# The start of an attention and gMLP kernel: first norms by a ScalarE root and a VectorE reciprocal, V weights in two pieces behind three chunks of x, turns woven into the first V passes

## Chip, cores, metric

One core of one Trainium2 chip. The metric is the device time of the whole kernel in microseconds (us). A run has a time and a mean granted TensorE clock (1.000 is full rate). Below, "T1" is the eight 128x128 transposes ("turns") of chunk 1 of x; a "pass" is one matmul of 512 columns; "wv a" and "wv b" are the two pieces of the V weights; "the fifth pass" is the first that needs wv b; "the first q pass" is the first matmul with the q weights, which follows all of the first V passes. TensorE takes its instructions in a fixed order, and so does each other engine.

## The reference

Layer norm of x, an attention with memory over four segments, a second layer norm and a gated MLP, 2048 rows of 1024. Only its first steps matter here: the norm of rows 0 to 511 (chunks 0 to 3 of 128 rows) and their product with the first 512 columns of wv.

```python
def _layernorm(x, axis=-1, eps=1e-05):
    m = jnp.mean(x, axis=axis, keepdims=True)
    v = jnp.var(x, axis=axis, keepdims=True)
    return (x - m) / jnp.sqrt(v + eps)
...
    x = A_x
    h = x + _A_ref(_layernorm(x, axis=-1), A_wq, A_wk, A_wv, A_wo, A_beta)
    h2 = h + _B_ref(_layernorm(h, axis=-1), B_w_in, B_w_sp, B_b_sp, B_w_out)
# in _A_ref: v = x @ wv, q = x @ wq, k = x @ wk, ...
```

## The kernel before

Every operation is recorded first. A list scheduler then lays down a fixed order for ScalarE (ACT), VectorE (DVE), GpSimd (POOL) and the DMA queue from assumed costs, while TensorE keeps the order of the program text. Its figures decide orders only; all times below are the chip's. These are the parts that the change touches:

```python
    N_WARM = 10
    AT = [5, 6, 6, 9]
    TCOPY = [(DVE, DVE), (ACT, ACT), (ACT, ACT), (DVE, ACT)]
    ...
    for k in range(N_WARM):
        mm(PS[:, 7, :], ZERO[:, 0:128], ZERO[:], True, True)
    ...
    for h in range(2):
        x_cols(0, h)                      # chunk 0 in two halves
    dma(XIN[1][:], x2d[128:256, :])
    wv_rows(0, 4)                         # wv a
    dma(XIN[2][:], x2d[256:384, :])
    wv_rows(4, 8)                         # wv b
    ...
    # layernorm(): bn_stats twice and bn_aggr on VectorE, then
        if start:
            ts1(RS[k][:], MV[k][:, 1:2], LN_EPS, ALU.add, fast=1)
        else:
            pts1(RS[k][:], MV[k][:, 1:2], LN_EPS, ALU.add)
        ptt(RS[k][:], RS[k][:], MHALF[:], ALU.pow)              # GpSimd
        ts(dst, src, MV[k][:, 0:1], RS[k][:], ALU.subtract, ALU.mult)
    ...
    # layernorm_act() (chunk 1): sum and sum of squares on ScalarE, then add and pow on GpSimd
    ...
    x_turn_pe(0)
    for tcl in range(4):
        b = bank()
        for i in range(8):
            if i == AT[tcl] and tcl < 3:
                x_turn_pe(tcl + 1)
            mm(b[:], XNT[0][:, i, tcl * 128:(tcl + 1) * 128], WV[:, i, 0:512], i == 0, i == 7)
        act(V[0][:, tcl, 0:16, 0:32], b.rearrange("p (h d) -> p h d", d=32), ACTF.Copy)

    for k, d in ((first[2], turned[0][1]), (first[2] + 1, first[1] + 4), (first[3], first[2] + 3),
                 (first[3] + 1, first[2] + 5)):
        G.ops[k].deps.add(d)              # e.g. chunk 2's first statistic behind chunk 0's copies
    Pq(0)
```

`AT[0] = 5` puts T1 behind chunk 0's fifth pass; `TCOPY` says which engine copies each half of a turn out of PSUM.

The softmax here doesn't subtract the row's maximum and nothing guards it: scores larger than these inputs give would overflow.

## Time and profile before

| | before |
|---|---|
| time, first three runs | 797.02 us median (796.05 to 797.2) |
| span of the profiled run | 795.0 us |
| TensorE busy | 789.5 us (99%) |
| wv b landed | 9.28 us |
| fifth pass starts | 9.32 us |
| first q pass starts | 16.97 us |

The span counts from the first to the last instruction. TensorE has hardly anything left to give, so the place to read is the chain of waits at the start. The lines are in the prediction below, with how to read them.

### The profile page before, as it was taken

How to read it: one execution, taken by the hardware profiler on the slowest of the kernel's cores; microseconds unless marked ns; L12 is line 12 of the kernel's file. 1: busy time of each engine (PE TensorE's matmuls, PEld its weight loads, DVE VectorE, ACT ScalarE, POOL GpSimd, SP SyncE). 2: the span in 40 equal slices, each digit the busy share in tenths (PEclk: the TensorE clock that was granted, in tenths of full speed). 3: DMA queues.
4: the chain of work that ended last, by engine and by line, in shares of the span. 5: the costliest groups of instructions: out<-in, count | busy, mean ns of one | idle time of the engine just before them, and what ended most of it. 6: DMA issues, size and time to landing. Idle time of an engine off the chain costs nothing.

```text
span 795.0 us, 12074 instructions
## 1 busy us (share of the span) xinstructions
PE 789.5 (99%) x5376; PEld 321.6 (40%) x4773; DVE 369.8 (47%) x853; ACT 288.6 (36%) x338; POOL 140.8 (18%) x270
## 2 busy tenths in 40 slices
PE   8999999999999999999999999999999999999998
PEld 3454554555554542341322414443244334424433
DVE  5773788768765686704215051132233223322322
ACT  4788977777778862132323323100000000000000
POOL 2463535433443341100001010000000000000000
DMA  9757524632523658420000116703310530011001
GB/s 307 156 123 172 137 47 95 136 68 68 87 55 87 173 117 216 145 53 1 1 0 1 28 33 157 187 1 82 105 33 1 119 100 1 0 54 60 0 1 54
DMA packets 128471, 64.77 MB, mean 81 GB/s; under 512 B 95520, under 2 KB 120352, under 8 KB 128416
## 3 DMA queue, kind: packets, MB, share of 16 engines
q1 hardware_dynamic: 128416, 63.99, 32.7%
q8 instruction: 40, 0.66, 0.3%
q14 instruction: 15, 0.12, 0.1%
HBM read 32.51 MB, written 8.39 MB: 51 GB/s over the span
## 4 chain that ended last, share of the span: by engine, by line
PE 99%; DMA 1%; SPq 0%; issue 0%; DVE 0%
PE ps L327 81%; PE ps L328 14%; PE ps L459 3%; DMA wv<-in_A_wv_dram 1%; SPq L511 0%; PE ps L463 0%; DVE hx L490 0%
## 5 line engine op out<-in xcount | busy, mean ns | idle before, releaser
L327 PE MATMUL ps<-wspT,z 128*128 128x512 bf16 x896 | 194.0, 379 | 0.0
L468 ACT ACTIVATE e<-ps 128x2048 bf16<-128x2048 f32 x80 | 149.8, 1873 | 40.0 <-PE ps L459 40.0
L327 PEld LDWEIGHTS ps<-wspT,z 128*128 128x128 bf16 x896 | 87.7, 98 | 106.4 <-issue 1.0
L468 ACT ACTIVATE z<-ps 128x512 bf16<-128x512 f32 x120 | 63.1, 571 | 145.4 <-PE ps L327 145.4
L490 DVE TENSOR_TENSOR tg<-ps,brow 128x512 bf16<-128x512 f32 x56 | 38.7, 691 | 150.2 <-PE ps L327 122.1
L693 POOL TENSOR_SCALAR_AFFINE_SELECT e<-e 128x1024 bf16<-128x1024 bf16 (+1 forms) x80 | 77.5, 969 | 122.5 <-ACT e L468 122.3
L327 PE MATMUL ps<-hnT,win 128*128 128x512 bf16 x448 | 97.3, 379 | 0.0
L328 PE MATMUL ps<-win,hnT 128*128 128x512 bf16 (+1 forms) x384 | 90.1, 344 | 0.0
L327 PE MATMUL ps<-wout,y 128*128 128x512 bf16 (+2 forms) x252 | 85.8, 367 | 0.0
L561 DVE BATCH_NORM_STATS2 stats<-z 128x6 f32<-128x448 bf16 x64 | 40.1, 627 | 96.6 <-ACT z L468 95.0
L490 DVE TENSOR_TENSOR hx<-hx,ps 128x512 bf16<-128x512 bf16 (+1 forms) x65 | 42.2, 673 | 81.7 <-PE ps L327 81.5
L328 PE MATMUL ps<-wout,y 128*128 128x512 bf16 x210 | 79.6, 379 | 0.0
L327 PEld LDWEIGHTS ps<-hnT,win 128*128 128x128 bf16 x448 | 43.9, 98 | 54.1 <-issue 2.0
L327 PE MATMUL ps<-wv,xnT 128*128 128x512 bf16 x256 | 60.7, 379 | 1.6 <-DMA wv<-in_A_wv_dram 1.3
L327 PE MATMUL ps<-xnT,wk 128*128 128x512 bf16 (+2 forms) x264 | 60.8, 374 | 0.0
L327 PE MATMUL ps<-xnT,wq 128*128 128x512 bf16 x256 | 60.8, 380 | 0.0
L327 PE MATMUL ps<-wo,oT 128*128 128x512 bf16 x256 | 58.8, 379 | 0.0
L327 PEld LDWEIGHTS ps<-wout,y 128*128 128x128 bf16 x252 | 24.2, 98 | 72.2 <-issue 69.1
L327 PE MATMUL ps<-win,hnT 128*128 128x512 bf16 x128 | 48.5, 379 | 0.0
L327 PEld LDWEIGHTS ps<-win,hnT 128*128 128x128 bf16 x128 | 12.5, 98 | 81.4 <-issue 80.9
L327 PEld LDWEIGHTS ps<-v,e 128*128 128x128 bf16 x1280 | 40.1, 96 | 9.8 <-issue 1.5
L327 PE MATMUL ps<-v,e 128*128 128x33 bf16 x1280 | 42.1, 177 | 0.0
(69 smaller groups left out, 604.3 us busy)
## 6 DMA issues: line engine op xcount, KB each, us to landing
win<-in_B_w_in_dram SPq DMA_DIRECT2D x6, 1024.0 KB, 5.7
hx<-in_A_x_dram SPq DMA_DIRECT2D x16, 256.0 KB, 3.0
out_dram<-hx SPq DMA_DIRECT2D x16, 256.0 KB, 2.3
hx<-out_dram SPq DMA_DIRECT2D x16, 256.0 KB, 2.8
out_dram<-hx SPq DMA_DIRECT2D x31, 128.0 KB, 1.7
xin<-in_A_x_dram SPq DMA_DIRECT2D x15, 256.0 KB, 5.2
wout<-in_B_w_out_dram SPq DMA_DIRECT2D x2, 1792.0 KB, 10.4
wq<-in_A_wq_dram SPq DMA_DIRECT2D x2, 1024.0 KB, 7.5
```

The source lines that it names most:

```text
L327: return e.matmul(out, lhsT, rhs, start=start, stop=stop)
L328: return e.add_instruction(mybir.InstMatmult(name="I-%d" % (1000000 + o.idx), engine=e.engine, ins=[e.lower_ap(rhs), e.lower_ap(lhsT)], ou ...
L459: G.op(PE, lambda e: e.matmul(o, lhsT, rhs, start=True, stop=True, tile_position=(32 * i, 0)), [lhsT, rhs], [o], n / 2.4 if last else 3.5, ...
L468: G.op(ACT, lambda e: e.activation(o, i, func, scale=scale, **kw), r, [o], ((172 if inps(i) else 224) + n_of(i)) / 1.2 + 26, prio=prio, na ...
L490: G.op(DVE, lambda e: e.tensor_tensor(o, a, b, op), [a, b], [o], vcost(o, [a, b], fast), name="tt", prio=late[0])
L561: G.op(DVE, lambda e, si=si, so=so: e.bn_stats(so, si), [si], [so], (cs + 143) / 0.96, name="bn_stats", prio=late[0])
L693: G.op(POOL, lambda e: e.affine_select(d, d, pat, ALU.is_ge, 0.0, base=0, channel_multiplier=-1), [d], [d], 1270 if j else 640, name="mask")
```

## The change

Its intent: make the first norms shorter, have x land ahead of the weights, and give TensorE something to do wherever a weight piece or a copy is late. The core of the diff:

```diff
-    N_WARM = 10
-    AT = [5, 6, 6, 9]
-    TCOPY = [(DVE, DVE), (ACT, ACT), (ACT, ACT), (DVE, ACT)]
+    N_WARM = 11
+    ON_ACT = (1,)
+    LOAD = '12ab3'
+    START = 'T00 t01 v00 v01 v02 v03 t10 T11 v04 v05 v06 v07 v10 v11 v12 v13 v14 T20 T21 v15 v16 v17 v20 v21 v22 v23 v24 T30 T31 v25 v26 v27 v30 ... v37'
+    AFTER = [(1, 1, 5)]
 ...
-    dma(XIN[1][:], x2d[128:256, :])
-    wv_rows(0, 4)
-    dma(XIN[2][:], x2d[256:384, :])
-    wv_rows(4, 8)
-    act(G1[:, 0:1], ZERO[:, 0:1], ACTF.Identity)
+    for c in LOAD:            # x1, x2, wv a, wv b, x3
+        ...
+    act(G1[:, 0:1], ZERO[:, 0:1], ACTF.Sqrt)
 ...
         if start:
-            ts1(RS[k][:], MV[k][:, 1:2], LN_EPS, ALU.add, fast=1)
+            act(RS[k][:], MV[k][:, 1:2], ACTF.Sqrt, bias=EPS[:])
+            recip(RS[k][:], RS[k][:])
         else:
             pts1(RS[k][:], MV[k][:, 1:2], LN_EPS, ALU.add)
-        ptt(RS[k][:], RS[k][:], MHALF[:], ALU.pow)
+            ptt(RS[k][:], RS[k][:], MHALF[:], ALU.pow)
 ... (chunk 1's norm likewise)
+        if x == "v27":        # load the exp table once the last root is done
+            G.op(ACT, lambda e: e.activation(G1[:, 0:1], RS[2][:], ACTF.Exp, scale=0.0), ...)
 ...
-    for k, d in ((first[2], turned[0][1]), (first[2] + 1, first[1] + 4), (first[3], first[2] + 3),
-                 (first[3] + 1, first[2] + 5)):
-        G.ops[k].deps.add(d)
+    for c, k, d in AFTER:
+        G.ops[first[c] + k].deps.add(...)
```

In START, t or T is half a turn (t copied by ScalarE, T by VectorE), v a pass; the first digit is the chunk. Two assumed transfer figures of the scheduler change as well.

More of the change, by code (lines that the diff above doesn't have):

```diff
@@ L213, in schedule @@
                 b = max(start + 1850.0, dma_free)
-                dma_free = b + o.nbytes / 350.0
-                o.t1 = dma_free + (700.0 if o.nbytes >= 200000 else 50.0)
+                dma_free = b + o.nbytes / 335.0
+                o.t1 = dma_free + (850.0 if o.nbytes >= 200000 else 100.0)
                 free[e] = start + cost
@@ L428, in bass_sequential_preLN__memory_aug_infini_attn__mixer_gmlp__prompt_kernel @@
     MHALF = tens("mhalf", [128, 1], F32)
+    EPS = tens("eps", [128, 1], F32)
     STATS = [tens("stats%d" % i, [128, 4, 6], F32) for i in range(4)]
@@ L433, in bass_sequential_preLN__memory_aug_infini_attn__mixer_gmlp__prompt_kernel @@
     RM = [tens("rm%d" % i, [128, 12], F32) for i in range(4)]
-    N_WARM = 10
-    AT = [5, 6, 6, 9]
-    TCOPY = [(DVE, DVE), (ACT, ACT), (ACT, ACT), (DVE, ACT)]
+    N_WARM = 11
+    ON_ACT = (1,)
+    LOAD = '12ab3'
+    START = 'T00 t01 v00 v01 v02 v03 t10 T11 v04 v05 v06 v07 v10 v11 v12 v13 v14 T20 T21 v15 v16 v17 v20 v21 v22 v23 v24 T30 T31 v25 v26 v27 v30 v31 v32 v33 v34 v35 v36 v37'
+    AFTER = [(1, 1, 5)]
     PS = nc.alloc_psum_tensor("ps", [128, 8, 512], F32)
@@ L536, in bass_sequential_preLN__memory_aug_infini_attn__mixer_gmlp__prompt_kernel @@
         x_cols(0, h)
-    dma(XIN[1][:], x2d[128:256, :])
-    wv_rows(0, 4)
-    dma(XIN[2][:], x2d[256:384, :])
-    wv_rows(4, 8)
-    act(G1[:, 0:1], ZERO[:, 0:1], ACTF.Identity)
+    for c in LOAD:
+        if c in "123":
+            dma(XIN[int(c)][:], x2d[int(c) * 128:int(c) * 128 + 128, :])
+        else:
+            wv_rows(*{"a": (0, 4), "b": (4, 8), "c": (4, 6), "d": (6, 8), "e": (0, 2), "f": (2, 4)}[c])
+    act(G1[:, 0:1], ZERO[:, 0:1], ACTF.Sqrt)
     iot = tens("iot", [128, 128], I32, R_E)
@@ L544, in bass_sequential_preLN__memory_aug_infini_attn__mixer_gmlp__prompt_kernel @@
     pset(MHALF[:], -0.5)
+    pset(EPS[:], LN_EPS)
     ts1(IDENT[:], iot[:], 0.0, ALU.is_equal)
@@ L578, in layernorm_act @@
              1250, name="sumsq")
-        G.op(POOL, lambda e: e.tensor_scalar(RS[k][:], ss, 1.0 / D, LN_EPS, ALU.mult, ALU.add), [ss], [RS[k][:]],
-             220, name="pts")
-        ptt(RS[k][:], RS[k][:], MHALF[:], ALU.pow)
+        act(RS[k][:], ss, ACTF.Sqrt, scale=1.0 / D, bias=EPS[:])
+        recip(RS[k][:], RS[k][:])
         ts(dst, src, nm, RS[k][:], ALU.add, ALU.mult)
@@ L603, in x_norm, with x_turn_pe @@
         layernorm(XIN[tc % 4][:], XIN[tc % 4][:], D, 600)
-    def x_turn_pe(tc):
+    def x_turn_pe(tc, h, eng):
         dst = XNT[0][:, :, tc * 128:(tc + 1) * 128]
-        for h in range(2):
-            bb = bank().bitcast(BF16)
-            for i in range(4):
-                c = 4 * h + i
-                tr(bb[:, i * 128:(i + 1) * 128], XIN[tc][:, c * 128:(c + 1) * 128])
-            bv = bb[:, 0:512].rearrange("p (c n) -> p c n", c=4)
-            if TCOPY[tc][h] == DVE:
-                late[0] = -200
-                copy(dst[:, 4 * h:4 * h + 4, :], bv)
-                late[0] = 0
-            else:
-                act(dst[:, 4 * h:4 * h + 4, :], bv, ACTF.Copy)
-            turned.setdefault(tc, []).append(len(G.ops) - 1)
+        bb = bank().bitcast(BF16)
+        for i in range(4):
+            c = 4 * h + i
+            tr(bb[:, i * 128:(i + 1) * 128], XIN[tc][:, c * 128:(c + 1) * 128])
+        bv = bb[:, 0:512].rearrange("p (c n) -> p c n", c=4)
+        if eng == DVE:
+            late[0] = -200
+            copy(dst[:, 4 * h:4 * h + 4, :], bv)
+            late[0] = 0
+        else:
+            act(dst[:, 4 * h:4 * h + 4, :], bv, ACTF.Copy)
     def x_turn(tc):
@@ L783, in wo_group @@
             dma(HNT[s][:, :, tcl * 128:(tcl + 1) * 128], hx[:], transpose=True)
-    x_load(3)
     w_half(WQ, A_wq, 0)
@@ L796, in bass_sequential_preLN__memory_aug_infini_attn__mixer_gmlp__prompt_kernel @@
         first.append(len(G.ops))
-        if tcl == 1:
-            layernorm_act(XIN[1][:], XIN[1][:], HX[0][:], 3)
+        if tcl in ON_ACT:
+            layernorm_act(XIN[tcl][:], XIN[tcl][:], HX[tcl % 2][:], (tcl + 2) % 4)
         else:
             layernorm(XIN[tcl][:], XIN[tcl][:], D, start=True)
-    turned = {}
-    x_turn_pe(0)
-    for tcl in range(4):
-        b = bank()
-        for i in range(8):
-            if i == AT[tcl] and tcl < 3:
-                x_turn_pe(tcl + 1)
-            mm(b[:], XNT[0][:, i, tcl * 128:(tcl + 1) * 128], WV[:, i, 0:512], i == 0, i == 7)
-        act(V[0][:, tcl, 0:16, 0:32], b.rearrange("p (h d) -> p h d", d=32), ACTF.Copy)
-    for k, d in ((first[2], turned[0][1]), (first[2] + 1, first[1] + 4), (first[3], first[2] + 3),
-                 (first[3] + 1, first[2] + 5)):
-        G.ops[k].deps.add(d)
+    turned, vb = {}, {}
+    for x in START.split():
+        c, i = int(x[1]), int(x[2])
+        if x[0] in "tT":
+            x_turn_pe(c, i, DVE if x[0] == "T" else ACT)
+            turned[c, i] = len(G.ops) - 1
+            continue
+        if i == 0:
+            vb[c] = bank()
+        b = vb[c]
+        mm(b[:], XNT[0][:, i, c * 128:(c + 1) * 128], WV[:, i, 0:512], i == 0, i == 7)
+        if i == 7:
+            act(V[0][:, c, 0:16, 0:32], b.rearrange("p (h d) -> p h d", d=32), ACTF.Copy)
+        if x == "v27":
+            G.op(ACT, lambda e: e.activation(G1[:, 0:1], RS[2][:], ACTF.Exp, scale=0.0), [RS[2][:]], [G1[:, 0:1]],
+                 1500, name="table")
+    for c, k, d in AFTER:
+        G.ops[first[c] + k].deps.add(turned[d] if isinstance(d, tuple) else first[d // 10] + d % 10)
     Pq(0)
```

## The prediction

> **What bounds the kernel now.** I read the head of the page first, then its chain that ended last, then the list of who waited for whom on the TensorE, then the timeline of the first 20 us. The page says how much room there is at all:
>
> ```profile
> span 795.0 us, 12074 instructions
> PE 789.5 (99%) x5376; PEld 321.6 (40%) x4773; DVE 369.8 (47%) x853; ACT 288.6 (36%) x338; POOL 140.8 (18%) x270
> PE 99%; DMA 1%; SPq 0%; issue 0%; DVE 0%
> ```
>
> TensorE (PE) is busy 789.5 of 795.0 us, so 5.5 us are idle in the whole run. Everything the change touches lies in the first 18 us. The waits of the TensorE over the whole span are only four:
>
> ```profile
> PE ps L327 <- DMA wv<-in_A_wv_dram: 1.3, 1, 1.3
> PE ps L327 <- DVE zero L526: 1.2, 1, 1.2
> PE ps L463 <- DVE xin L484: 0.4, 1, 0.4
> PE ps L327 <- DVE xnT L480: 0.3, 1, 0.3
> ```
>
> Each line is who waited, for what, us in total, times, longest. They sum to 3.2 us; the other 2.3 us are the tail after the last matmul (the window from 400 us to the end has 392.73 busy of 395), which the change doesn't touch. The 1.2 us wait is the start of the program, before the zero tile exists, and is not touched either. So at most 1.3 + 0.4 + 0.3 = 2.0 us, 0.25% of the span, can be won, and even this only if the transfers allow it. The chain in order of time says which of the three counts:
>
> ```profile
> 2.65 0.50 SPq L511
> ...
> 3.20 6.08 DMA wv<-in_A_wv_dram
> 9.28 0.04 issue
> 9.32 0.39 PE ps L327
> 9.71 0.45 PE ps L463 x8
> 10.16 1.94 PE ps L327 x9
> ```
>
> Columns are start, length, what. The chain runs over six issues on the DMA queue, then the second piece of wv, issued at 3.20 and landed at 9.28, and from there TensorE runs without a wait to the end. The 0.4 and 0.3 us waits lie before 9.28 and are therefore hidden: the wait for wv would only be longer without them. What counts is how much TensorE work remains to be done after wv's second piece has landed. The timeline before that point:
>
> ```profile
> 1.64 4.03 PE L328 MATMUL ps<-zero 128*128 128x512 bf16 x9
> 4.92 0.55 POOL L500 TENSOR_TENSOR rs<-rs,mhalf 128x1 f32<-128x1 f32 x1 [2.33 <-DVE rs L487]
> 6.11 0.62 PE L463 MATMUL ps<-ident,xin 128*128 128x128 bf16 x8 [0.44 <-DVE xin L484]
> 7.03 1.04 PE L327 MATMUL ps<-wv,xnT 128*128 128x512 bf16 x4 [0.29 <-DVE xnT L480]
> 9.32 0.39 PE L327 MATMUL ps<-wv,xnT 128*128 128x512 bf16 x1 [1.26 <-DMA wv<-in_A_wv_dram]
> 9.55 0.61 PE L463 MATMUL ps<-ident,xin 128*128 128x128 bf16 x8
> ```
>
> Ahead of the landing TensorE does the eight transposes (turns) of chunk 0 and its first four V passes, then idles 1.26 us. It can't do the turns of chunk 1 there, since in TensorE's fixed order the fifth V pass, which needs the second piece, stands before them.
>
> **What the Trainium skill says.** "ScalarE: Activation LUTs", section "What ACT_TABLE_LOAD costs", gives 1283 ns for a table load (and a drain); the trace has 1283 ns for each of its two loads, at 0.78 us and for the gelu at 293.5. The same section gives 186 ns plus 0.833 ns per element for an activation, and about 280 ns with a pointer bias; the trace's one-element activation took 204 ns, and no row here has a one-element one with a pointer, so 0.28 us is my estimate for a square root from that page. The section "Table sets: the hidden batching unit" says square root and exp are in different sets while cheap functions are in every one; the trace before can't show it, having no square root. "TensorE: Matmul & The Clock Gate", section "What's actually happening", has the array at half rate until about 3.4 us of sustained work. The trace agrees: 10 warm matmuls of 512 columns, from 1.24 to the end of the last at 5.67, are about 0.43 us apart, the eight turns at 6.11 are 0.45/8 = 0.056 us apart, and later passes 0.22.
>
> **The change part by part.**
>
> Chunk 0's norm. It removes the add (0.15 us) and the power on GpSimd (0.55): from the end of the aggregate, 4.43 + 0.21 = 4.64, to the start of the scaling at 5.51 are 0.87 us. It adds a square root (0.28) and a reciprocal. The trace has a reciprocal only of 32 elements, 0.35 us; for one element I take 0.16, like the 0.154 us add of the same size. With three hand-overs of about 0.05, as in these rows, that is 0.28 + 0.16 + 0.15 = 0.59, so scaling starts near 5.24 and ends near 5.79, about 0.28 earlier. The eleventh warm matmul, at 0.43, ends the cold row's issue near 1.24 + 11 x 0.427 = 5.94. So chunk 0's turns start near 5.95 and not at 6.11. This fills most of the 0.44 us wait but isn't on the chain.
>
> The transfers. Order before: x0, x1, wv a, x2, wv b, x3. After: x0, x1, x2, wv a, wv b, x3. Issue and landing before, from the issues taken one by one: x1 1.71 + 3.3 = 5.0; wv a 2.17 + 4.5 = 6.7; x2 2.65 + 5.2 = 7.85; wv b 9.28; x3 3.68 + 6.3 = 9.98. The bytes ahead of wv b are the same, 1.25 MB, so its landing stays near 9.28. x2 comes right behind x1: 256 KB at some 305 to 358 GB/s (4 to 6 us) are 0.8 us, so near 5.9. wv a then takes the place of x2's landing, near 7.8.
>
> The first V passes. They now start with wv a near 7.85 instead of 7.03, and four of them are issued in 4 x 0.217 = 0.87, to about 8.7. Nothing is lost: before, TensorE idled from 7.9.
>
> The turns of chunk 1. They now stand before the fifth V pass. Are they ready? ScalarE sums chunk 1 from 5.07 to 7.50 in both versions (x1's landing is unchanged and the square root of chunk 0, 4.70 to 4.98, fits ahead). The root of chunk 1 is then done near 7.8. In VectorE's order I expect, from the program's priorities, chunk 2's first statistic (from x2's landing, 5.93 to 6.62), chunk 0's first copy (0.42, to 7.07), the second statistic (0.69, to 7.79), the aggregate (0.21, to 8.03), the reciprocal (to 8.2) and chunk 1's scaling (0.55, 8.24 to 8.78). The turns go from about 8.85 to 9.30, just before wv b has landed. So 0.45 us of work leaves the stretch after 9.32. If x2 lands 0.3 us later, the turns end 0.3 later and the gain is about 0.15.
>
> After that. Turn 2 is wanted by TensorE near 11.26 (four passes for chunk 0, five for chunk 1, 9 x 0.216) and chunk 2 is ready before 9.5. Turn 3 is wanted near 11.26 + 0.45 + 8 x 0.216 = 13.4; x3 lands at 9.98, two statistics, the aggregate, two copies of turn 2 (0.42 each, from about 11.7), the reciprocal and the scaling put it near 13.25: just in time. The exp table load, 1.28 us, comes after chunk 3's root, near 12.9 to 14.4 on ScalarE, with a V copy before it and the next wanted only near 14.7. It stays beside TensorE.
>
> Sum: 0.45 from the turns, less 0.05 for small hand-overs and a chance of a short wait at turn 3: 0.4 us of 797.0.
>
> **The rivals.**
> 1. All 2.0 us of waits vanish and the time goes to 795.0. For it: three parts of the change aim at these waits. Against: the chain goes through wv b's transfer, whose bytes ahead are unchanged, and only 0.45 us of turns move in front of it. To win more, wv b would have to land earlier.
> 2. The root becomes the wait. If the squares of chunk 1 needed another table than the root, two more loads of 1.28 us would sit in chunk 1's path on ScalarE, and the turns, which now block the fifth pass, would start near 11.4 and not 8.85: about 2 us lost, 799. For it: the turns are now ahead of the pass in a fixed order. Against: the trace before runs Identity, Square, Copy and Exp with a single load until 293 us, as cheap fillers would.
> 3. VectorE becomes the bound of the start: x2 or x3 later than I think, so chunk 1's or chunk 3's turns come 0.3 to 0.5 us late. It would leave 797.0 to 797.2. VectorE's statistics, at 0.69 us each, are the long pieces here.
> 4. The changed transfer figures in the program's own scheduler alter the order on ScalarE and VectorE in the attention part, with a few short waits: up to 1 us lost. Against: before, TensorE has no wait from 9.3 to 792 us, so there is slack.
>
> **Range and chances.** The three runs before span 796.05 to 797.2, so noise of about 0.6 either way is more than the gain. From 797.0 - 0.4 = 796.6, and a little for the case that the transfers come out better, I predict 796.5 us. Rivals 3 and 4 and noise give the upper end, 797.4; rival 1 in part and noise the lower, 795.5. Over 2% faster is 781 us, below the 789.5 us of TensorE's busy time, so impossible short of a different clock: 0.005. Slower by 2% would be 813: 0.005. Within 2%: 0.99.
>
> **What would show it right or wrong.** Span near 794.6. In the timeline: the first root right behind the aggregate and scaling near 5.2; first turns near 5.95; x2's statistics from about 5.9; a wait for wv a ending near 7.8; sixteen turns issued before wv b's pass at about 9.3; no wait of more than 0.1 us after it; three table loads. The prediction is wrong if wv b lands more than 0.3 us from 9.28, if the turns of chunk 1 end after 9.6, if a fourth table load appears, or if TensorE shows waits beyond 20 us.

## The result

| | before | changed |
|---|---|---|
| median of six runs, us | 796.75 | 796.27 |
| lowest to highest, us | 796.05 to 797.2 | 795.97 to 796.97 |
| span of the profiled run, us | 795.0 | 794.5 |
| fifth pass starts, us | 9.32 | 9.52 |
| first q pass starts, us | 16.97 | 16.46 |
| last matmul done, us (chain) | 792.75 | 792.24 |

The ratio is 0.9996, with a 95% interval of 0.9983 to 1.0009. A ratio is the mean time of one kernel's fast runs over that of the other's of the same rounds, so not quite the ratio of the medians. The times alone can't tell the two apart; the traces can, up to a point. The page of the changed kernel, for the first lines of that of before:

```profile
span 794.5 us, 12077 instructions
PE 789.9 (99%) x5377; PEld 322.2 (41%) x4773; DVE 373.1 (47%) x857; ACT 289.8 (36%) x341; POOL 140.1 (18%) x266
```

TensorE's waits in the changed kernel (who, for what, us in total, times, longest):

```profile
...
PE ps L327 <- DMA wv<-in_A_wv_dram: 1.1, 2, 0.7
```

The waits for x and for its copy, 0.4 and 0.3 us before, are gone. There are two waits for wv now, 0.7 and 0.35, where there was one of 1.26. The chain in order of time (start, length, what) still goes through wv b:

```profile
3.12 6.35 DMA wv<-in_A_wv_dram
...
9.52 2.12 PE ps L327 x9
```

After the fifth pass come nine passes in a row; the eight turns that stood second in the chain before are no longer behind the landing. The timeline of the changed kernel shows where they went:

```profile
4.61 0.29 ACT L473 ACTIVATE rs<-mv,eps 128x1 f32<-128x1 f32 x1 [2.34 <-DVE mv L571]
4.94 0.17 DVE L502 RECIPROCAL rs<-rs 128x1 f32<-128x1 f32 x1 [0.36 <-ACT rs L473]
5.90 1.06 PE L468 MATMUL ps<-ident,xin 128*128 128x128 bf16 x8
7.68 1.04 PE L327 MATMUL ps<-wv,xnT 128*128 128x512 bf16 x4 [0.71 <-DMA wv<-in_A_wv_dram]
8.55 0.61 PE L468 MATMUL ps<-ident,xin 128*128 128x128 bf16 x8
9.52 2.12 PE L327 MATMUL ps<-wv,xnT 128*128 128x512 bf16 x9 [0.35 <-DMA wv<-in_A_wv_dram]
...
16.46 1.89 PE L327 MATMUL ps<-xnT,wq 128*128 128x512 bf16 x8
```

Root and reciprocal take 0.29 and 0.17 us. The eight turns of chunk 0 at 5.90 take 1.06 us against 0.62 before: the array was still at half rate there, ahead of the wait for wv a, where it costs nothing. (The granted clock of the views doesn't show this slow start: it is 1.00 from 0 to 7 us.) T1 starts at 8.55, and TensorE still idles 0.35 us after it. The third table load, from 13.38 to 14.66 us on ScalarE, lies beside TensorE.

Now the sum. From the fifth pass to the first q pass are 16.97 - 9.32 = 7.65 us before and 16.46 - 9.52 = 6.94 after, so 0.71 less. T1 is 0.45 of it; 0.26 is unexplained. Against that, wv b landed 0.19 us later. The net is 0.51, which is the change of the span, and it stays to the last matmul (792.75 against 792.24). My prediction had the net and not the two other terms. What stands there in the kernel before, between chunk 2's turns and the next passes:

```profile
12.37 1.08 ACT L468 ACTIVATE xnT<-ps 128x512 bf16<-128x512 bf16 x2 [0.81 <-PE ps L463]
12.39 2.10 PE L327 MATMUL ps<-wv,xnT 128*128 128x512 bf16 x8
13.01 0.98 PEld L327 LDWEIGHTS ps<-wv,xnT 128*128 128x128 bf16 x6 [0.53 <-ACT xnT L468]
```

Two passes are issued at 12.39 and 12.60; the third wants a weight that ScalarE copies from 12.37 to 12.97, and its load starts at 13.01. Passes come 0.216 us apart, so the third should start at 12.82. The page shows no idle TensorE there, because the modelled length of a pass, 0.38 us, covers the hole. A hidden wait of 0.2 us is my guess for the missing part.

### The profile page after: what moved, and what is told of

The parts are those of the page before. It is cut to its first block, busy times and chain, and to the rows that moved or that the text cites. A ratio compares the mean times of both kernels' runs of the same rounds, so it can differ in the third digit from the quotient of the medians.

```text
span 794.5 us, 12077 instructions
## 1 busy us (share of the span) xinstructions
PE 789.9 (99%) x5377; PEld 322.2 (41%) x4773; DVE 373.1 (47%) x857; ACT 289.8 (36%) x341; POOL 140.1 (18%) x266
## 4 chain that ended last, share of the span: by engine, by line
PE 99%; DMA 1%; SPq 0%; issue 0%; DVE 0%
PE ps L327 81%; PE ps L328 14%; PE ps L464 3%; DMA wv<-in_A_wv_dram 1%; SPq L516 0%; PE ps L468 0%; DVE hx L495 0%
```

## The experiments

My theory: what counts is the TensorE work left when wv b has landed. T1's move takes 0.45 us out of it, the wider gap between a turn and the pass that needs it takes out some 0.2, and roots and transfer order only shorten what is hidden. The rivals: the faster root gains the time; the order of transfers does; or it is all scatter. The figure to read in each trace is the distance from the fifth pass to the first q pass, which is free of the landing's scatter. It leaves out what happens between the landing and the fifth pass, so where T1 holds the fifth pass back, read the distance from the landing too (7.69 us before, 6.99 in the changed kernel).

### The changed kernel again, twice (a_again, a_third)

No edit.

> The changed kernel once more, to see how much the landing of wv's second piece and the place of the first q pass vary between executions. The first pass with the q weights started at 16.97 us before and 16.46 after; the second wv piece landed at 9.28 before and 9.47 after. If the 0.19 us between the landings is scatter, this run's landing lies anywhere within 9.2 to 9.6 and the q pass follows it one for one (landing + 6.99). If it belongs to the new order of transfers, it is 9.4 to 9.5 again. Time: within 0.1% of before, 0.4 to 0.6 us less.

> The changed kernel a third time, for the share of its executions that are 2 us longer. In the second study of it two of five executions took 798.3 us with a mean granted clock of 0.998, against 796.2 to 796.6 of the other three; of the kernel before none of 12 did. 0.002 of 796 us is 1.6 us: about one stretch of 3.3 us at half rate. If this is a property of the changed kernel, I expect one or two of these five near 798.3; if it was chance, none. Also one more landing of wv's second piece, anywhere in 9.2 to 10.5, with the first q pass 6.94 us behind the fifth pass.

In the first, wv b landed at 9.74, the fifth pass started at 9.79 and the first q pass at 16.73: again 6.94 us. So the distance is firm and the landing is not (9.74 is outside the 9.2 to 9.6 that I gave). But two of its five times were 798.36 and 798.32 us, with a clock of 0.998. In the second, three of six were (798.78, 797.88, 798.39), and the profile fell on one of these. TensorE's timeline in that trace, with the weight load of the first V passes, the passes and T1:

```profile
8.59 0.55 PEld L327 LDWEIGHTS ps<-wv,xnT 128*128 128x128 bf16 x4 [1.89 <-DMA wv<-in_A_wv_dram]
8.60 1.04 PE L327 MATMUL ps<-wv,xnT 128*128 128x512 bf16 x4 [1.63 <-DVE stats L568]
9.90 0.67 PE L468 MATMUL ps<-ident,xin 128*128 128x128 bf16 x8 [0.26 <-DVE xin L489]
```

And one stretch of it from the table by windows (the window, its length, busy time and count of PE, PEld, DVE, ACT and POOL, then granted clock, DMA share, GB/s):

```profile
10.30:13.70 3.40, 3.40 (x12) 1.28 (x10) 2.13 (x5) 1.38 (x3) 0.00 (x0) 0.50 1.10 350
```

x1 and x2 landed late in this execution (4.6 and 4.8 us after their issue, against 2.8 and 3.0 in the first trace of the same kernel). VectorE's fixed order has chunk 2's statistic ahead of chunk 0's copy, so the copy waited for x2; the dependencies that the change dropped had held the statistic behind it. But the copy ended at 7.98, and wv a landed only at 8.55 (2.65 + 5.9): though the line of the passes names VectorE, the weight load shows that they waited for wv a. T1 came at 9.90 and not at 8.55, behind chunk 1's norm and so behind x1, and the fifth pass followed it at 10.36, 0.3 us after wv b. TensorE idled 1.63 us, and soon after, from about 10.3 to 13.7, the clock was at half rate. The first q pass came at 18.98, 8.62 us behind the fifth pass and not 6.94 as expected: the 1.7 more are half of these 3.4 us. The five disturbed runs of the changed kernel average 798.35, some 2.0 us above the others, so the clock makes up most of it. They are less than 1.5% above the rest; so I separate by clock. Over all results:

| | runs | at clock 1.000 | mean of these, us | below 1.000 |
|---|---|---|---|---|
| before | 29 | 28 | 796.69 | 1 (799.66) |
| changed | 17 | 12 | 796.34 | 5 (797.88 to 798.78) |

(For the first six of before no clock is listed run by run; none was above 797.2.) Undisturbed, the change gains 0.35 us, with single runs spread over about 1 us; in none of the three comparisons does the recorded interval of the ratio exclude 1. With the disturbed runs counted, the means are 796.79 before and 796.93 changed: nothing. Chance alone would give a split as uneven as 5 of 17 against 1 of 29 about one time in fifty.

### T1 put back (a_turn_back)

```diff
-... v02 v03 t10 T11 v04 v05 ...
+... v02 v03 v04 t10 T11 v05 ...
```

> The changed kernel with chunk 1's turns put back behind the fifth pass of chunk 0, all else kept. My theory (the turns that moved ahead of the landing are 0.45 us of the gain): the TensorE does 0.45 us more after the landing, so the distance from the landing to the first q pass grows from 6.99 to about 7.45 us and the gain over before falls to about 0.05 us. Rival (the faster root is what gains): unchanged distance, 6.99 us, since the roots and reciprocals stay.

This gave 797.99 us, ratio 1.002 (1.0006 to 1.0035). Three of six runs were disturbed (800.72, 799.47, 798.93), the profiled one most. TensorE's timeline in that trace, at the landing of wv b:

```profile
10.51 0.61 PE L327 MATMUL ps<-wv,xnT 128*128 128x512 bf16 x1 [2.29 <-DMA wv<-in_A_wv_dram]
```

Two stretches of the same trace, in the table by windows (granted clock third from the end):

```profile
9.80:13.10 3.30, 2.59 (x13) 1.49 (x14) 1.75 (x4) 0.60 (x1) 0.00 (x0) 0.50 1.09 367
13.10:16.40 3.30, 3.30 (x15) 1.71 (x14) 0.73 (x3) 0.78 (x2) 0.00 (x0) 0.50 1.10 348
```

wv b landed at 10.46, the wait was 2.29 us, and the clock was at half for twice 3.4 us, from 9.7 to 16.5. The distance can't be read from this trace. The three undisturbed runs, 796.92, 797.06 and 796.92, average 796.97, which is 0.63 above the changed kernel's undisturbed mean; I had expected 0.45. The direction fits the theory and not the rival, since the roots were kept. The distance was measured in the next run.

### T1 put back, and the waits filled (a_turn_back_fill)

```diff
-T00 t01 v00 v01 v02 v03 t10 T11 v04 v05
+T00 t01 w w v00 v01 v02 v03 w w w w v04 t10 T11 v05
```

w is one pass over zeros into a free PSUM bank, as in the warm-up.

> The same test where the slow executions were most frequent (three of six with chunk 1's turns back behind the fifth pass, 798.9 to 800.7 us, the others 796.92 to 797.06): two passes over zeros in the first wait and four in the second. Theory: none above 797.6, and in the trace, undisturbed now, 6.94 + 0.45 = 7.39 us from the fifth pass to the first q pass, which is what that run could not show as its clock had fallen to half. If idle time is not the cause, two or three of five are slow again.

TensorE's timeline, the fifth pass and the first q pass:

```profile
10.53 0.39 PE L327 MATMUL ps<-wv,xnT 128*128 128x512 bf16 x1 [1.32 <-DMA wv<-in_A_wv_dram]
...
17.92 1.89 PE L327 MATMUL ps<-xnT,wq 128*128 128x512 bf16 x8
```

The distance is 7.39 us, as expected to the last digit: T1 alone is worth 0.45. The landing was as late as in the run above (10.48 against 10.46), yet no clock fell: five of five runs at 1.000 (796.79 to 797.73; the highest is just above the bound of 797.6 I had set, at full clock).

### The changed kernel with filled waits (a_fill)

```diff
-T00 t01 v00 v01 v02 v03 t10 T11 v04 v05
+T00 t01 w w v00 v01 v02 v03 t10 T11 w w v04 v05
```

> The changed kernel with two passes over zeros where the TensorE waits for wv's first piece and two where it waits for the second. Theory of the slow executions: the granted clock falls to half because the TensorE stands idle too long around the two waits; with the idle stretches filled none of the five is above 797.5, and all lie in 796.0 to 797.0, since the four passes (0.22 us each at full rate) fit into the waits of 0.4 to 1.2 us. If the slow executions come from elsewhere, one or two are near 798.3 again. If the fillers do not fit, the fifth pass starts after the landing by more than 0.1 us.

Six of six at clock 1.000, again as the theory has it: 11 of 11 filled runs undisturbed, where the same two orders without fillers had 8 of 23 disturbed. Chance alone would give that about one time in 37, so the runs point to idle TensorE around the two waits as what lets the clock fall. The traces fit it: in the 3.41 us before the fall TensorE was busy 1.51 us in a_third (6.92 to 10.33) and 1.48 in a_turn_back (6.29 to 9.70), while in the twelve traces at full clock no stretch of that length between 3.5 and 17 us has less than 1.60 (least in b_turn2_earlier, 6.18 to 9.59; 2.34 in the first trace of the changed kernel). Two falls are too few for a rule. "TensorE: Matmul & The Clock Gate", section "HAM oscillation — how this bites in real kernels", tells of such a fall after waits for DMA; the trace agrees in kind. But the filled kernel isn't faster: the profiled run took 796.25, the other five 797.0 to 797.5, where I had expected 796.0 to 797.0. In the profiled trace wv b landed at 8.78, T1 was issued by 8.98 and the fillers by 9.41, so there they held the fifth pass for 0.43 us, against my bound of 0.1. Whether the same holds for the other five no trace shows.

### T1 moved in the kernel before, alone (b_turn_ahead)

```diff
-    AT = [5, 6, 6, 9]
+    AT = [4, 6, 6, 9]
```

> The kernel before with chunk 1's turns alone moved ahead of the fifth pass of chunk 0 (the power on GpSimd and the order of transfers stay). Chunk 1's scaling ended at 9.03 there, so its turns run from about 9.1 to 9.55 and the fifth pass starts at 9.57, not 9.32: of 0.45 us moved, 0.25 are lost again to waiting for the norm. Theory: first q pass near 16.97 - 0.20 = 16.77. If the norm's speed did not matter at all, 16.52; if the turns did not matter, 16.97.

TensorE's timeline, with T1, the fifth pass and the first q pass:

```profile
8.94 0.62 PE L463 MATMUL ps<-ident,xin 128*128 128x128 bf16 x8 [0.92 <-DVE xin L484]
9.40 2.32 PE L327 MATMUL ps<-wv,xnT 128*128 128x512 bf16 x10
...
16.58 1.89 PE L327 MATMUL ps<-xnT,wq 128*128 128x512 bf16 x8
```

The distance is 7.18, and 7.65 - 7.18 = 0.47: T1's part, without roots and without the new transfer order. From the landing (9.22) it is 7.36 instead of 7.69, so 0.33 were gained in this execution. Its q pass came earlier than I said (16.58 against 16.77), since chunk 1 was ready sooner and wv b landed near 9.2. T1 now waits for chunk 1's norm, not for wv, so here a faster norm could gain something, up to the 0.2 us between landing and fifth pass. Time: 796.56 us, ratio 1.0000 (0.9987 to 1.0012).

### Chunk 2's turns one pass earlier in the kernel before (b_turn2_earlier)

```diff
-    AT = [5, 6, 6, 9]
+    AT = [5, 5, 6, 9]
```

All engines but TensorE keep their order to the instruction.

> The kernel before with chunk 2's turns one pass earlier (three passes rather than two between them and the first pass that needs their copies; VectorE, ScalarE and the rest in the same order). From the landing to the first q pass there were 7.69 us before and 6.99 after, 0.70 less, of which the moved turns explain 0.45. I suspect that the other 0.2 is a wait of the TensorE for ScalarE's copy of chunk 2's turns, near 13.0 us, that the page shows only as 0.03 us of issue because the modelled ends of matmuls cover it. If so: the first q pass comes 0.2 us earlier, near 16.77, and the next weight load after chunk 2's turns no longer waits for ScalarE's xnT. If not: 16.97 as before.

TensorE's timeline, the fifth pass and the first q pass:

```profile
9.59 0.39 PE L327 MATMUL ps<-wv,xnT 128*128 128x512 bf16 x1 [1.52 <-DMA wv<-in_A_wv_dram]
...
17.02 1.67 PE L327 MATMUL ps<-xnT,wq 128*128 128x512 bf16 x7
```

The distance is 7.43 instead of 7.65: 0.22 less, so the hidden wait was there and this was its size. (In the changed kernel VectorE makes both copies of T2, in 0.42 us each where ScalarE took 0.60, so there the faster copies may have closed the same hole; no run separates the two.) The q pass itself was at 17.02, not at the 16.77 I wrote, because wv b landed 0.26 later in this execution. I had forgotten the scatter when I wrote a time instead of a distance. Time: 797.04 us, ratio 1.0004 (0.9992 to 1.0016); the times don't show the gain.

### The power back on GpSimd in the changed kernel (a_pow_norm)

```diff
-            act(RS[k][:], MV[k][:, 1:2], ACTF.Sqrt, bias=EPS[:])
-            recip(RS[k][:], RS[k][:])
+            ts1(RS[k][:], MV[k][:, 1:2], LN_EPS, ALU.add, fast=1)
+            ptt(RS[k][:], RS[k][:], MHALF[:], ALU.pow)
```

and the same in chunk 1's norm.

> The changed kernel with the power on GpSimd put back in the place of root and reciprocal for all four chunks (table loads, order of transfers and interleaving kept). Theory (the root only shortens work that is hidden): chunk 0's scaling starts at about 5.4 instead of 5.14, chunk 1's ends near 8.8 instead of 8.46, its turns end near 9.3, still before the second wv piece at 9.47, so the distance from landing to first q pass stays at 6.99 us within 0.1. The one risk is chunk 3: its scaling ended at 13.31 and its turns began at 13.64, so up to 0.3 us later costs nothing. Rival (the root is the gain): the distance grows by 0.3 us or more.

TensorE's timeline, the fifth pass and the first q pass:

```profile
9.64 2.12 PE L327 MATMUL ps<-wv,xnT 128*128 128x512 bf16 x9
...
16.65 1.89 PE L327 MATMUL ps<-xnT,wq 128*128 128x512 bf16 x8
```

T1 started at 9.11, 0.56 later than with the root, its last turn was issued by about 9.56, and the fifth pass started at 9.64 (wv b landed near 9.6). The distance is 7.01 us, so the root's 0.56 us at T1 are worth 0.07 at the first q pass. Some 0.22 more were lost near 20.4 us: the scheduler had laid ScalarE's order anew, with a step on beta ahead of the copies of q and k, and beta landed at 19.48. That is a side effect of the edit and not the norm's speed. Time: 796.65 us, four of four at clock 1.000; ratio 0.9998 (0.9984 to 1.0013). The rival of the root has fallen for executions in which wv b lands as here; where it lands earlier, the power on GpSimd can hold T1 and cost something, as the trace of b_both below shows.

### The old order of transfers in the changed kernel (a_load_before)

```diff
-    LOAD = '12ab3'
+    LOAD = '1a2b3'
```

> The changed kernel with the transfers in the order of before (x1, wv a, x2, wv b, x3). If the new order causes the later landing, wv b lands near 9.28 again; if it is scatter, anywhere within 9.2 to 9.6. x2 lands near 7.85, not near 5.2, and VectorE, in its fixed order, has chunk 2's statistics then; if these stand ahead of chunk 1's scaling in its order, chunk 1's turns come near 9.5 to 9.9 and the first q pass is up to 0.4 us later than 16.46; if they stand behind it, the turns end before 9.3 and the q pass is near 16.3.

wv b landed near 9.70, so the old order doesn't make it land earlier here, and the 0.19 us of the first comparison lie within the scatter. Over all traces with the same bytes in front, wv b landed at 9.12 to 9.70 in the old order (five traces, mean 9.37) and at 8.78 to 10.48 in the new one (eight, mean 9.75). So few don't show a later landing in the new order, nor exclude it. The first q pass came at 17.44, 7.69 after the fifth pass at 9.75, so 0.75 were lost, and not at T1, as I had thought possible: T1 was issued at 8.48. The loss is at chunk 3. ScalarE's timeline there:

```profile
13.00 0.60 ACT L473 ACTIVATE v<-ps 128x512 bf16<-128x512 f32 x1 [1.58 <-PE ps L327]
13.49 0.28 ACT L473 ACTIVATE rs<-mv,eps 128x1 f32<-128x1 f32 x1
```

TensorE's timeline, T3:

```profile
14.61 0.62 PE L468 MATMUL ps<-ident,xin 128*128 128x128 bf16 x8 [0.57 <-DVE xin L489]
```

Chunk 3's aggregate was done at 13.00, but the root stands behind a V copy in ScalarE's fixed order and starts at 13.49. T3 waits 0.57 us for the scaling, and the passes behind it move as well. VectorE's order has a part too: chunk 3's statistics were done at 11.83, but the aggregate stands behind T2's two copies, which in the changed kernel come after it (aggregate at 11.65). The scheduler laid these orders from its assumed transfers. So x2's place does matter to the changed kernel, but this run shows it also through the order that the scheduler made of it; that the landing of x2 alone would do it isn't shown. Time: 797.28 us, ratio 1.0007 (0.9994 to 1.0019).

### x2 behind both pieces of wv (a_x2_last)

```diff
-    LOAD = '12ab3'
+    LOAD = '1ab23'
```

> The changed kernel with x2 behind both pieces of wv, so that wv b lands earlier by x2's 256 KB. Landing expected at 9.47 - 0.7 = 8.8 us; if only that landing counted, the first q pass would be near 15.8. But x2 then lands near 9.4 and its norm (two statistics of 0.69, aggregate 0.21, root 0.29, reciprocal 0.15, scaling 0.55, hand-overs) ends near 11.9 to 12.1, while the TensorE wants chunk 2's turns near 8.8 to 9.0 + 9 x 0.216 = 10.9: I expect a wait of about 1 us there, and the first q pass at 16.6 to 17.2. This tells whether x2's early place is what keeps chunk 2 off the path.

wv b landed near 8.25 (issued at 2.65, 5.6 us). The fifth pass started at 9.38 behind T1 at 8.92, which waited 0.99 us for chunk 1's norm; T2 waited 0.62 for chunk 2's and T3 0.57 for chunk 3's; the first q pass came at 17.85. I had expected the wait at T2 and not the other two, so the result lies above my range of 16.6 to 17.2. Over 1 us of earlier weights bought nothing: the norms took their place. Time: 797.27 us, ratio 1.0008 (0.9995 to 1.0021).

### T2 ahead of the landing too (a_turn2_ahead)

```diff
-... t10 T11 v04 v05 v06 v07 v10 v11 v12 v13 v14 T20 T21 v15 ...
+... t10 T11 T20 T21 v04 v05 v06 v07 v10 v11 v12 v13 v14 v15 ...
```

> An attempt to beat both: the turns of chunk 2 too stand ahead of the fifth pass of chunk 0. Chunk 2's scaling ended at 9.11 in the changed kernel, so its turns can run from about 9.15 to 9.6, where the TensorE waits for wv b until 9.47 now. Theory (what lies behind the landing is what counts): 0.45 us leave the stretch, 0.08 to 0.1 come back since the turns end after the landing: the first q pass at about 16.46 - 0.35 = 16.1, span about 794.1. If it stays at 16.46, another wait (chunk 3's norm, VectorE's copies) has taken its place.

TensorE's timeline, with T1 and T2 together, the fifth pass and the first q pass:

```profile
8.57 1.29 PE L468 MATMUL ps<-ident,xin 128*128 128x128 bf16 x16 [0.47 <-DVE xin L489]
9.69 3.83 PE L327 MATMUL ps<-wv,xnT 128*128 128x512 bf16 x17
...
16.29 1.89 PE L327 MATMUL ps<-xnT,wq 128*128 128x512 bf16 x8
```

The distance is 6.60, 0.34 less, but the sixteen turns end only at about 9.67, after the landing (9.39). From the landing it is 6.90 against 6.99, so 0.09 of the 0.45 moved were gained. The q pass is 0.17 earlier than in the first trace of the changed kernel, not 0.35, and half of that is the earlier landing. Times: 796.09, 796.55, 796.62 at full clock, and 798.58 at 0.998. It doesn't stand out from the changed kernel.

### Two passes moved in the kernel before (b_both)

```diff
-    AT = [5, 6, 6, 9]
+    AT = [4, 5, 6, 9]
```

> The kernel before with two passes of the order moved and nothing else: chunk 1's turns ahead of the fifth pass and chunk 2's turns one pass earlier. Alone they made the stretch from the fifth pass to the first q pass 7.18 and 7.43 us instead of 7.65. If they add up, it is 6.94 to 7.0 us, the same as in the changed kernel, with the norms on GpSimd and the order of transfers of before; first q pass at 16.3 to 16.5 if wv lands by 9.4. None of the six single runs of the two was slow, so I expect all five in 795.9 to 796.9, median 796.3, that is as fast as the changed kernel without its slow executions. If chunk 2's norm is late (it ended at 11.41, wanted at about 11.34), up to 0.1 us comes back.

(The text on record counts six runs of the two single moves; there were ten, none with a fallen clock.) TensorE's timeline, the fifth pass and the first q pass:

```profile
9.58 2.11 PE L327 MATMUL ps<-wv,xnT 128*128 128x512 bf16 x9
...
16.55 1.89 PE L327 MATMUL ps<-xnT,wq 128*128 128x512 bf16 x8
```

The distance is 6.97, against 6.94 in the changed kernel: the two moves add up and make the whole of that difference. But the chain in order of time (start, length, what) no longer goes through wv b. It goes through chunk 1's norm:

```profile
7.93 0.57 POOL rs L500
...
9.12 0.62 PE ps L463 x8
```

wv b had landed at 9.12, so T1, held by the norm on GpSimd, kept the fifth pass back by 0.4 us. From the landing to the first q pass are 7.43 us, against 7.69 before and 6.99 in the changed kernel, whose T1 started at 8.5 to 8.6 in its two undisturbed traces. So the moves are the gain where wv b lands at 9.5 or later; where it lands earlier, the faster norm can have its share. Five of five runs at clock 1.000, 796.36 to 796.89, median 796.47 (expected 796.3); ratio 0.9994 (0.9982 to 1.0007). The mean, 796.58, is 0.11 below before's and 0.24 above that of the changed kernel's undisturbed runs: these runs resolve neither, so that two digits are as fast as the whole change isn't shown. None of the fifteen runs of the three kernels with such edits was disturbed (of before 1 of 29 was).

## Why the prediction was right or wrong

The number was right: 796.5 predicted, 796.27 measured, inside 795.5 to 797.4; span 794.6 predicted, 794.5 measured. By its steps:

- **The bound** (the chain through wv b, and the work left behind it) holds in the first two traces of the changed kernel. Where wv b lands early (8.78 in a_fill) or x1 late (a_third), the chain goes through chunk 1's norm instead. The waits of 0.4 and 0.3 us ahead of the landing disappeared without being worth anything, as was said.
- **T1 is worth 0.45 us**: measured twice as a distance (0.47 in the kernel before, 0.45 with T1 put back and filled); the times of three undisturbed runs, 0.63, point the same way.
- **The turns are ready**: said 8.85, measured 8.55. The root was sized right (0.28 said, 0.29 measured). The reciprocal took 0.17 (0.16 said). x2 landed at 5.2, not at 5.9.
- **The half-rate start** was longer than the 3.4 us that the prediction found the trace to agree with: passes are 0.43 us apart from 1.24 to at least 5.05 in that trace, and in the first changed one the turns at 5.90 still run at half pace. It varies: in b_turn_ahead the ten warm passes end at 4.86, not at 5.67.
- **"Its landing stays near 9.28"** was too firm. The same bytes in front, and wv b landed between about 8.8 and 10.5 in the traces that kept them, and a_again, with 9.74, broke the bound of 0.3 us that the prediction set itself. The difference of 0.19 between the first two traces is well inside that.
- **"From there TensorE runs without a wait to the end"** was the reading that failed. 0.22 us of waiting for ScalarE's copy of chunk 2's turns was in the kernel before, and the sum lacked this term. It cancelled the later landing, so part of the prediction's precision was luck.
- **The rivals**: the 2.0 us of rival 1 did not appear, nor a table load for each square (rival 2; three loads in all, as said). Rival 3 appeared in one execution, a_third, in the form of a late x1 that held chunk 1's turns until 9.90, with more harm than the 0.2 us it was given. Rival 4 did not show: TensorE has no wait beyond 20 us in the changed kernel's first trace.
- **What was missing**: that a longer wait also costs the clock. About one execution of the changed kernel in three (5 of 17) is some 2 us longer, 1.7 of it by the clock. The six runs of the first comparison had none.

Still open: how much idle time, and where, lets the clock fall (a gap of 1.52 us in the trace of b_turn2_earlier did not; 1.63 and 2.29 elsewhere did; the busy time of the 3.41 us before it, 1.5 us against 1.6 and more, parts them, but barely); and why the changed kernel has more such executions than before (a later landing in the new order of transfers is one candidate, untested). One trace shows late x chunks at work, but the other timed runs have no traces.

## What to carry to other kernels

When an engine is 99% busy and one transfer gates it, count the work that is still to be done behind that landing, and move work in front of it; two digits shortened that stretch here as much as a page of edits did. Then ask what the moved work waits for itself: with the slower norm T1 held up the fifth pass in both traces in which the weights came early. Leave several passes between a turn and the pass that needs its copy, and look for such holes in the starts of the matmuls, not in the idle column. Look at the granted clock of single runs as well as at the median: a wait that is longer in some executions can cost as much again in clock.

## What the Trainium skill lacked or had wrong

- "TensorE: Matmul & The Clock Gate", section "HAM oscillation — how this bites in real kernels", gives the rule of no idle gap over some 3.4 us. Here the clock fell to half after gaps of 1.63 us (with shorter ones around it) and 2.29 us, for one and for two stretches of 3.4 us, with TensorE busy 1.5 us of the 3.41 us before, and 11 of 11 runs with the gaps filled kept it.
- "ScalarE: Activation LUTs", section "What ACT_TABLE_LOAD costs", adds a drain of about 1380 ns to a load. In the changed kernel the activation before the exp load ended at 13.36, the load ran from 13.38 for 1.28 us, and the next activation started at 14.67: no such drain. The figure for a one-element activation with a pointer bias, about 280 ns, agrees (0.29).
- No page that I found gives the scatter of a landing between executions: x1 behind the same two halves of chunk 0 took 2.8 to 4.6 us from issue to landing, and wv b 5.7 to 7.4 us.
